# The last pair's memory stage in its own order, and the expert slots opened one attention group sooner

## The chip, the cores and the metric

One core of a Trainium2 chip runs the whole program. Its engines are TensorE (matmuls, called PE in the rows; PEld is its weight load), VectorE (DVE), ScalarE (ACT) and GpSimd (POOL); SyncE (SP) issues most transfers. Each engine works through its own queue strictly in the order of the program, and waits for others by semaphores. The metric is the device time of one execution in microseconds (us), the median of three runs.

## The reference

Eight batches with eight heads of 576 tokens attend to 32 memory slots per head; the 4608 output rows of 512 go through a top-1 mixture of eight experts. Cut to what matters:

```python
a = softmax(phi, axis=tokens)                       # phi: [8, 8, 576, 32]
k_m, v_m = a^T k, a^T v                             # "memory": 32 rows of 64 per head
attn = softmax(q k_m^T / sqrt(64)) v_m              # [8, 8, 576, 64]
x = attn as [4608, 512]
e_idx = argmax(x @ w_gate); gate_w = its softmax probability
eom = sigmoid(x @ w_output_gate)
out[mask_e] = gate_w * eom[:, e] * (relu(x[mask_e] @ w1[e]) @ w2[e])
```

## The kernel before

**Attention stage.** The batches go in four pairs (`bp` 0 to 3). For each pair the generator `memory(bp)` computes k_m and v_m (and v_m times the gate weights) from nine chunks of 128 tokens, for the two batches ("halves") of the pair. The order of its steps is a hand-written tuple, one letter and a number per step: `a` turns chunks of phi (TensorE transposes, ScalarE copies), `s` adds chunks to the sums in PSUM (32 small matmuls for a pair of chunks, 8 and 9 being the two parts of the last chunk), `p` spreads a finished half, `t` transposes it, `g` and `v` make its gate columns, `x` is a step of the next pair's softmax, and `.` gives the word back to the attention loop. `MEM0` orders pair 0 and `MEM` all others.

The loop `attention()` walks 20 groups (five per pair, of 256 tokens of four heads twice, the fifth of 64) through stages that lag each other: scores one group ahead (`C`, line 838), subtract the maximum, exponential, divide, transpose back (`B`), and values three groups later (`V`, line 899), stored to DRAM (line 1002). Each letter of `ORDER` is one step, and some of them take a step of memory or of routing along.

**Routing.** When a pair's logits are there, `rank` numbers its tokens per expert. After pair 1 `route_early` makes the early list (table "a": compares on VectorE at line 232, 72 small matmuls on TensorE at line 242, then indices), from which slots 0 to 3 gather their tokens. After pair 3 `route_late` makes the late list (table "l", 144 matmuls). `hold(n)` keeps a step back for n ticks of a program-time clock; `LATE` has those numbers for the time when slots are open.

**Expert stage.** A slot is up to 576 tokens of one expert. Its tokens come by five indirect row gathers issued by GpSimd (line 441), are transposed by TensorE (lines 1136, 1141) and split into a high and a low part (line 1099), as are the weights (ScalarE line 537, VectorE line 542). Slots 0 to 2 run as `plain`: 16 banks of 12 matmuls each (line 1310), evicted by ScalarE (1276) and VectorE (1281), and then the second layer (line 1442), five output tiles. Between banks a `hook` takes three attention steps and two of routing along, until attention is through.

Where the experts begin, and where the pools of routing are closed, is set by these lines:

```python
while t == START - 2 and stream.split(2):      # first weights are split
yield "open" if w == "S" and t == START else None   # the slots begin here
if t == START - 1:
    mem.finish()
if (i, step) == OPEN:                          # (2, 2): slot 2, third hook
    reopen()                                   # late.finish(), pools close
```

Of the kernel before, what the change touches and what calls it, by code (L numbers as in the profile page):

```python
# [19 lines left out]
NBP = B // 2  # L20
# [16 lines left out]
LAG = {"X": 1, "B": 2, "D": 1, "V": 3, "C": -1}  # L37
TICK = 0
HOOK = (3, 2)
START = 17  # L40
SWAP = ()
NKV = 8
NQ = 3
# [3 lines left out]
NLD = 2  # L47
MEM = ("a8", "a0", ".", "a2", ".", ".", "s0", ".", "a4", "s2", "x", "x", ".", ".", "s8", ".", "p0", "a6", ".", "x", ".", "s4", "x", "t0", ".", ".", "s9", "g0", "v0", ".", "s6", ".", "x", ".", "p1", "x", ".", "t1", ".", ".", "g1", "v1", ".")
MEM0 = ("a0", "s0", ".", "a2", "a8", ".", "s2", ".", "s8", "p0", "a4", ".", ".", "t0", ".", "g0", "a6", ".", "v0", "s9", "s4", ".", "s6", ".", ".", "p1", ".", "t1", "x", "x", ".", "g1", "x", ".", "v1", "x", ".", "x", ".", "x", ".", ".")
NPK = 1  # L50
PHI1 = 6
NEA = 3
LATE = {"lg": 8, "w": 2, "pe": 3, "dve": 2}
GROW = ((4, 0, 0), (2, 0, 0), (0, 2, 0))
SOON = {"pe": 3, "dve": 0, "tab": 12, "w": 3, "ix": 2}
PACE = 30
# [27 lines left out]
def attention_moe(tc, phiT, kv, qT, wgo, wall, out):  # L84
# [3 lines left out]
    with contextlib.ExitStack() as ctx:  # L88
# [134 lines left out]
        def table(nm, q, nch, nblk):  # L223
# [12 lines left out]
            yield from take_pr()  # L236
            yield from hold(LATE["pe"], SOON["tab"])
            pi = ps_r.tile([P, NBL], F32, name="pr")
# [5 lines left out]
            yield  # L244
            yield from hold(LATE["dve"], SOON["ix"])
            i2 = rt.tile([P, NBL], F32, name="i2")
# [9 lines left out]
        def route_early(n_):  # L256
# [27 lines left out]
            def slots_early():  # L284
# [6 lines left out]
                known(*order[0:NPE])  # L291
                yield from hold(LATE["w"], SOON["w"])
                stream.fetch()
# [96 lines left out]
        def take_pr():  # L390

            while taken:
                yield
            taken.append(1)

        def hold(n, soon=0):

            end = clock[0] + (n if "open" in env else soon)
            while clock[0] < end:
                yield  # L400
# [60 lines left out]
        def known(*zs):  # L461
            for z in zs:
                z["known"] = True
# [131 lines left out]
        ld = pl.enter_context(tc.tile_pool(name="ld", bufs=2, side="right"))  # L595
        ps_k = prr.enter_context(tc.tile_pool(name="ps_k", bufs=NPK, space=PSUM))
        pso = contextlib.ExitStack()
        env["pa"] = pso.enter_context(tc.tile_pool(name="pa", bufs=3 - NPK, space=PSUM))
        env["pd"] = pso.enter_context(tc.tile_pool(name="pd", bufs=2, space=PSUM))
# [66 lines left out]
        def soften(bp):  # L666

            ph = phs[bp]
            nmx = sm.tile([P, 4], F32, name="nmx")
            ssum = sm.tile([P, 4], F32, name="ssum")  # L670
            o = (0, 2, 1, 3)
            for i in range(5):
                if i < 4:
                    x = o[i]
                    V.tensor_reduce(nmx[:, x:x + 1], ph[:, x], axis=AX.X, op=ALU.max, negate=True)
                    tick()
                if i:
                    x = o[i - 1]
                    A.activation(ph[:, x], ph[:, x], AF.Exp, bias=nmx[:, x:x + 1], accum_out=ssum[:, x:x + 1])
                yield  # L680
            rs = sm.tile([P, 4], F32, name="rs")
            V.tensor_scalar(rs[:], ssum[:], 1e-9, None, ALU.add)
            V.reciprocal(rs[:], rs[:])
            rss[bp] = rs
            yield

        def memory(bp):
# [5 lines left out]
            a8 = ld.tile([P, 2, 256], F32, name="a8", bufs=1)  # L693
# [4 lines left out]
            def turn_a(*chunks):  # L698
                pt = bank([2, 256])
                for k, c in enumerate(chunks):  # L700
                    for g in range(2):
                        o = 512 if c == 8 else c * P + (c // 4) * P
                        T.transpose(pt[:, k, g * P:(g + 1) * P], exg[:, g, o:o + P], ident[:])
                c = chunks[0]
                turned.remove(c)
                if not turned and bp + 2 < NBP:
                    load_phi(bp + 2)
                if c == 8:
                    A.copy(a8[0:64, 0], pt[0:64, 0])
                    A.copy(a8[64:128, 1], pt[64:128, 0])  # L710
                else:
                    t = ld.tile([P, 2, 256], F32, name="at", bufs=NAT)
                    A.copy(t[:], pt)
                    at[c], at[c + 1] = t[:, 0], t[:, 1]
# [6 lines left out]
            def sums(c):  # L721

                b = 1 if c in togo[1] else 0
                if len(togo[b]) == 3:
                    z[b]["pk"] = ps_k.tile([P, 2, 2 * D], F32, name="pk")
                    T.matmul(z[b]["pk"][:].rearrange("p g d -> p (g d)"), zero[:, 0:P], zero[:],
                             start=True, stop=False)
                pk = z[b]["pk"]
                for ca_ in (c,) if c >= 8 else (c, c + 1):
                    for g in range(2):  # L730
                        for h in range(4):
                            T.matmul(pk[32 * h:32 * h + 32, g],
                                     at[ca_][:, g * P + 32 * h:g * P + 32 * h + 32],
                                     kvts[bp, min(ca_, 8)][:, 4 * g + h],
                                     start=False, stop=False)
                togo[b].remove(c)
                if not togo[b]:
                    T.matmul(pk[:].rearrange("p g d -> p (g d)"), zero[:, 0:P], zero[:], start=False, stop=True)
                if c < 8:
                    lod.step()  # L740
                elif b and bp + 1 < NBP:
                    load_kv(bp + 1, 8)

            def spread(b):

                z[b]["kv"] = kvm = ld.tile([P, 2, 2 * D], F32, name="kvm", bufs=2)
                z[b]["ve"] = wk.tile([P, 2, XQ], F32, name="ve_b", bufs=4)
                for g in range(2):
                    A.activation(kvm[:, g], z[b]["pk"][:, g], AF.Copy, scale=rs[:, 2 * g + b:2 * g + b + 1])
                h2 = [P, 2, 2, D]  # L750
                G.tensor_tensor(z[b]["ve"][:, :, 0:P].rearrange("p g (h d) -> p g h d", h=2),
                                kvm[:, :, D:2 * D].unsqueeze(2).to_broadcast(h2),
                                hmask[:].unsqueeze(1).unsqueeze(3).to_broadcast(h2), ALU.mult)
# [26 lines left out]
            def room():  # L780

                while len(ves) >= 4 + 2 * len(left):
                    yield

            soft = soften(bp + 1) if bp + 1 < NBP else iter(())
            for w in MEM if bp else MEM0:
                c = w[1:]
                if w == ".":
                    yield
                elif w[0] == "a":  # L790
                    turn_a(*((8,) if c == "8" else (int(c), int(c) + 1)))
                elif w[0] == "s":
                    sums(int(c))
                elif w[0] == "p":
                    yield from room()
                    spread(int(c))
                elif w[0] == "t":
                    turn_kv(int(c))
                elif w[0] == "g":
                    gates(int(c))  # L800
                elif w[0] == "v":
                    gates2(int(c))
                elif w == "x":
                    next(soft, None)
# [98 lines left out]
        def rank(bp, lg):  # L903
# [55 lines left out]
            def main():  # L959
                yield from take_pr()  # L960
                yield from hold(LATE["pe"], SOON["pe"])

# [10 lines left out]
                yield  # L973
                yield from hold(LATE["dve"], SOON["dve"])
                V.tensor_tensor(w1_[:], oh, pr[:, 0:NCH], ALU.mult)
# [171 lines left out]
        def defer(nm, f):  # L1147
            deferred.append([LATE[nm], f])

# [14 lines left out]
        def attention():  # L1164
# [8 lines left out]
            for t in range(NT + LAG["V"]):  # L1173
                for w in ORDER:
# [8 lines left out]
                    elif w == "W":  # L1183

                        while t == START - 2 and stream.split(2):
                            pass
# [29 lines left out]
                    clock[0] += 1  # L1216
                    yield "open" if w == "S" and t == START else None
                g = t - LAG["V"]
                if g >= 0 and g % 5 == 4:
# [6 lines left out]
                    else:  # L1226
                        late.gens.append(rank(bp, lgs[bp]))
                if t == START - 1:
                    mem.finish()
# [285 lines left out]
        def settle():  # L1515
# [6 lines left out]
            grow(1)  # L1522
            env["ps"] = prp.enter_context(tc.tile_pool(name="p1", bufs=7 - NPK, space=PSUM, reuse_waits="tile"))

# [59 lines left out]
        pso = contextlib.ExitStack()  # L1584
        env["ps"] = pso.enter_context(tc.tile_pool(name="p0", bufs=5 - NPK, space=PSUM, reuse_waits="tile"))
        env["pd"] = pso.enter_context(tc.tile_pool(name="pd1", bufs=1, space=PSUM, reuse_waits="tile"))
# [55 lines left out]
```

## Time and profile before

| | |
|---|---|
| median of 3 runs | 541.02 us (540.85 to 543.61) |
| profiled execution, its own time | 543.56 us |
| its span, first to last instruction | 541.6 us, so 2.0 us lie around it |
| TensorE busy | 506.0 us, 93% |
| VectorE, ScalarE, GpSimd busy | 375.6, 280.9, 164.8 us |
| mean granted TensorE clock | 0.964 of full |
| DMA | 104.01 MB, mean 192 GB/s |

The profile is of one execution; its time is that of the slowest of the three runs, and its rows are read for durations and order. The share of an engine is an average over the attention stage, in which TensorE has idle time, and the expert stage.

### The profile page before, as it was taken

Reading aid. Unit: us, or ns where it says so; the run is one execution under the profiler, and the core shown is the slowest. Engines: PE = TensorE matmul, PEld = TensorE weight load, DVE = VectorE, ACT = ScalarE, POOL = GpSimd, SP = SyncE. Lnnn points to the kernel's source line nnn. Section 1 sums busy time; section 2 is a strip of 40 time slices with the busy share of each in tenths; the row PEclk is TensorE's granted clock in tenths of the full one; section 3 lists DMA queues with packets and bytes.
Section 4 is the critical chain, followed back from the end, with each engine's and each line's share of the span. In section 5 each row is a group of like instructions: output and inputs, shape, how many; then the busy total and the mean of one; then the engine's idle time right before and its main releaser. Section 6 shows DMA issues by size and latency. Waiting matters only on the chain. (4 is left out here: it accounts for less than half of the span.)

```text
span 541.6 us, 11081 instructions
## 1 busy us (share of the span) xinstructions
PE 506.0 (93%) x4205; PEld 429.5 (79%) x4205; DVE 375.6 (69%) x870; ACT 280.9 (52%) x535; POOL 164.8 (30%) x168
## 2 busy tenths in 40 slices
PE   3788886989999999999999999999999999999995
PEld 2455554769877898789988988998898899889983
DVE  4374889787942698545593898688789878978600
ACT  4475764265533453244264756665574666548311
POOL 2242554543421330214146114302621341130021
PEclk9977998599999999999999999999999999999999
DMA  8999999888353664218407832980594188130011
GB/s 317 424 392 386 413 412 398 289 308 254 128 170 110 213 224 125 88 50 322 87 12 229 268 78 72 304 209 8 178 267 133 45 292 216 36 95 34 0 50 45
DMA packets 42111, 104.01 MB, mean 192 GB/s; under 512 B 4992, under 2 KB 16576, under 8 KB 41664
## 3 DMA queue, kind: packets, MB, share of 16 engines
q1 hardware_dynamic: 36160, 83.15, 46.0%
q0 software_dynamic: 5888, 20.06, 10.8%
q8 instruction: 35, 0.57, 0.4%
q14 instruction: 28, 0.23, 0.1%
HBM read 77.23 MB, written 20.05 MB: 180 GB/s over the span
## 5 line engine op out<-in xcount | busy, mean ns | idle before, releaser
L1442 PE MATMUL bps<-whl,hh 128*128 128x512 f32 x560 | 170.4, 398 | 0.0
L542 DVE TENSOR_TENSOR whl<-w,whl 128x1024 fp32r<-128x1024 f32 x74 | 90.7, 1233 | 48.6 <-ACT whl L537 40.2
L1442 PEld LDWEIGHTS bps<-whl,hh 128*128 128x128 f32 x560 | 104.7, 188 | 24.7
L1442 PE MATMUL bps<-whl,hl 128*128 128x512 f32 x216 | 85.4, 395 | 0.0
L537 ACT CAST whl<-w 128x1024 fp32r<-128x1024 f32 x74 | 76.8, 1049 | 4.3 <-PE bpc L1442 2.8
L1310 PE MATMUL bps<-xh,whl 128*128 128x288 f32 x384 | 77.6, 298 | 0.0
L1310 PEld LDWEIGHTS bps<-xh,whl 128*128 128x128 f32 x384 | 61.5, 188 | 1.3 <-DVE gr L1061 0.4
L1267 POOL DMA_INDIRECT out<-y,idx_oa x20 | 26.0, 1300 | 105.3 <-ACT y L1266 80.9
L1310 PE MATMUL bps<-xl,whl 128*128 128x288 f32 x192 | 54.8, 296 | 0.0
L1267 POOL DMA_INDIRECT out<-y,idx_ol x20 | 22.7, 1137 | 104.0 <-ACT y L1266 70.5
L1338 PE MATMUL bpc<-xh,whl 128*128 128x288 f32 x240 | 49.4, 296 | 0.0
L1338 PE MATMUL bpc<-th,whl 128*128 128x288 f32 x240 | 49.3, 295 | 0.0
L1442 PEld LDWEIGHTS bps<-whl,hl 128*128 128x128 f32 x216 | 40.7, 188 | 9.3
L1266 ACT ACTIVATE y<-bps,gx 128x512 f32<-128x512 f32 x27 | 18.6, 689 | 44.7 <-PE bps L1442 39.8
L1276 ACT ACTIVATE hh<-bps 128x288 fp32r<-128x288 f32 x48 | 19.7, 411 | 39.9 <-PE bps L1310 38.8
L1338 PEld LDWEIGHTS bpc<-xh,whl 128*128 128x128 f32 x240 | 38.9, 188 | 0.2
L1338 PEld LDWEIGHTS bpc<-th,whl 128*128 128x128 f32 x240 | 39.0, 188 | 0.0
L1276 ACT ACTIVATE hh<-keep 128x288 fp32r<-128x288 f32 x60 | 26.7, 445 | 22.7 <-DVE keep L1349 22.7
L901 ACT COPY xo<-bpd 128x576 f32<-128x576 f32 x36 | 22.2, 641 | 28.1 <-issue 9.5
L1310 PEld LDWEIGHTS bps<-xl,whl 128*128 128x128 f32 x192 | 35.6, 188 | 0.2
L857 POOL TENSOR_TENSOR ea<-ea,mx 128x512 f32<-128x512 f32 (+1 forms) x18 | 17.6, 977 | 59.5 <-DVE mx L855 51.3
L1338 PE MATMUL bpc<-tl,whl 128*128 128x288 f32 x120 | 35.4, 295 | 0.0
(246 smaller groups left out, 950.3 us busy)
## 6 DMA issues: line engine op xcount, KB each, us to landing
w<-wall SPq DMA_DIRECT2D x64, 512.0 KB
kvt<-kv SPq DMA_DIRECT2D x32, 512.0 KB
xs<-xo SPq DMA_DIRECT2D x16, 576.0 KB
qt<-qT SPq DMA_DIRECT2D x16, 512.0 KB
ph<-phiT SPq DMA_DIRECT2D x3, 1152.0 KB
xq<-xg SPq DMA_DIRECT2D x40, 80.0 KB
xq<-xg SPq DMA_DIRECT2D x40, 64.0 KB
kv<-kv SPq DMA_DIRECT2D x4, 512.0 KB
```

Of the source, the lines that this page charges most:

```text
L537: A.copy(hl[:, 0], w[:])
L542: V.tensor_tensor(hl[:, 1], w[:], hl[:, 0].bitcast(F32), ALU.subtract)
L857: (V if z["k"] in BESIDE[0] else G).tensor_tensor(eav, eav, mx[:, 0:n].unsqueeze(2).to_broadcast([P, n, M]), ALU.subtract)
L901: A.copy(xo[:, c % 2], px[:, :, 0:2 * XQ])
L1266: A.activation(y[0:n], py[0:n], AF.Copy, scale=z["g"][0:n, k:k + 1])
L1267: G.indirect_dma_start(out=out, out_offset=bass.IndirectOffsetOnAxis(ap=z["idx"][1][0:n, z["q0"] + k:z["q0"] + k + 1], axis=0), in_=y[0:n] ...
L1276: A.activation(h_[:, j, c:e], src, AF.Relu)
L1310: T.matmul(pb, w[:, b, o:o + P], x[a][:, cc, c * SL // 2:(c + 1) * SL // 2], start=(n == 0), stop=(n == 11))
L1338: T.matmul(pb, w[:, b, o:o + P], z[x][a][:, kc], start=(first and n == 0), stop=(n == 5), skip_group_check=not first)
L1442: T.matmul(py, a, w[:, b, DM * f:DM * f + DM], start=(u == 4 and f == 0 and n == 0), stop=(u == 7 and f == 1 and n == len(ps) - 1))
```

## The change

Three numbers or orders change. Pair 3 gets a tuple `MEM3` of its own: without the softmax steps of a next pair, with fewer pauses, and with `s9`, `s4` and `t0` in an earlier place. `START` goes from 17 to 16, so the slots open one group sooner and one group more is done in the hooks of slot 0. `LATE["pe"]` goes from 3 to 5 ticks, for the matmuls of `rank` and of the late table. As one line is added, line numbers of the change are one higher.

```diff
-START = 17
+START = 16
...
+MEM3 = ("a8", "a0", ".", "a2", ".", ".", "s0", ".", "a4", "s2", ".", "s8", ".", "p0", "a6", ".", "s9", "s4", "t0", ".", "g0", "v0", "s6", ".", "p1", ".", "t1", ".", "g1", "v1", ".")
...
-LATE = {"lg": 8, "w": 2, "pe": 3, "dve": 2}
+LATE = {"lg": 8, "w": 2, "pe": 5, "dve": 2}
...
-            for w in MEM if bp else MEM0:
+            for w in MEM3 if bp == NBP - 1 else MEM if bp else MEM0:
```

The order that it replaces for pair 3 (the `x` steps do nothing there):

```python
MEM = ("a8", "a0", ".", "a2", ".", ".", "s0", ".", "a4", "s2", "x", "x", ".", ".", "s8", ".", "p0", "a6", ".", "x", ".", "s4", "x", "t0", ".", ".", "s9", "g0", "v0", ".", "s6", ".", "x", ".", "p1", "x", ".", "t1", ".", ".", "g1", "v1", ".")
```

**Place 1.** TensorE ahead of the early list's table (the rows of Aw), in pair 3's memory stage; before. `ph` is phi, `at` and `a_1279` its turned chunks, `kvt` and `kv_1147` chunks of k and v, `pk` the sums, `kvm` a spread half.

```order
L732 MATMUL pk<-kvt,at 32x128 x16
L899 MATMUL bpd<-ve_b,aT 128x144 x8
L732 MATMUL pk<-kv_1147,a_1279 32x128 x8
L738 MATMUL pk<-zero 128x256
L703 MATMUL bpa<-ident,ph 128x128 x4
L838 MATMUL bpd<-qt,kT_177 32x64 x8
L838 MATMUL bpd<-qt,kT_178 32x64 x8
L242 LDWEIGHTS Aw
```

The same place of the change:

```order
L733 MATMUL pk<-kvt,at 32x128 x16
L733 MATMUL pk<-kv_1147,a_1279 32x128 x8
L739 MATMUL pk<-zero 128x256
L900 MATMUL bpd<-ve_b,aT 128x144 x8
L704 MATMUL bpa<-ident,ph 128x128 x4
L727 MATMUL pk<-zero 128x256
L733 MATMUL pk<-kv_1147,a_1279 32x128 x8
L733 MATMUL pk<-kvt,at 32x128 x16
L759 MATMUL bpa<-ident,kvm 128x128 x2
L839 MATMUL bpd<-qt,kT_177 32x64 x8
L839 MATMUL bpd<-qt,kT_178 32x64 x8
L243 LDWEIGHTS Aw
```

The second half's first sums (chunk 9, chunks 4 and 5) and the first half's transposes have come ahead of the table.

**Place 2.** TensorE from the end of the table to slot 0's first token transposes (`xg` are the gathered tokens); before, with the zero matmul's rows left out.

```order
L899 MATMUL bpd<-ve_b,aT 128x144 x8
...
L732 MATMUL pk<-kvt,at 32x128 x16
L758 MATMUL bpa<-ident,kvm 128x128 x2
L838 MATMUL bpd<-qt,kT_179 32x256 x8
L732 MATMUL pk<-kv_1147,a_1279 32x128 x8
L772 MATMUL bpa<-wg,vT_b 32x16 x8
L899 MATMUL bpd<-ve_b,aT 128x144 x8
L732 MATMUL pk<-kvt,at 32x128 x16
...
L899 MATMUL bpd<-ve_b,aT 128x144 x8
L772 MATMUL bpa<-wg,vT_b 32x16 x8
L838 MATMUL bpd<-qt,kT_180 32x256 x8
L1136 MATMUL bps<-ident,xg 128x128 x4
```

The same place of the change:

```order
L773 MATMUL bpa<-wg,vT_b 32x16 x8
L733 MATMUL pk<-kvt,at 32x128 x16
...
L900 MATMUL bpd<-ve_b,aT 128x144 x8
L839 MATMUL bpd<-qt,kT_179 32x256 x8
L759 MATMUL bpa<-ident,kvm 128x128 x2
L773 MATMUL bpa<-wg,vT_b 32x16 x8
L900 MATMUL bpd<-ve_b,aT 128x144 x8
L839 MATMUL bpd<-qt,kT_179 32x256 x8
L1137 MATMUL bps<-ident,xg 128x128 x4
```

One group's values and one group's scores are gone from here (they follow inside slot 0), and the sums of place 1. In SyncE's queue the second two weight loads now stand right behind the second store after the table, ahead of one load of q and one store.

**Place 3.** VectorE at the compares of the late list (`eql`), which TensorE's 144 matmuls read; before, where they stand at the end of slot 1.

```order
L378 TENSOR_TENSOR q_3063<-q_3063,q_3104 128x36
L232 TENSOR_TENSOR eql<-iota_bl,q_3063 128x864 x4
L542 TENSOR_TENSOR whl<-w,whl 128x1024
L1080 MEMSET lx 64x16
L1081 TENSOR_REDUCE lx<-xg 64x16
```

In the change, where they stand among slot 2's first evictions:

```order
L1282 SCALAR_TENSOR_TENSOR hl<-bps,hh 128x288
L1052 TENSOR_REDUCE gr<-lx 128x5
L1053 TENSOR_TENSOR ex<-iota_s,slot 128x8
L233 TENSOR_TENSOR eql<-iota_bl,q_3093 128x864 x2
L1282 SCALAR_TENSOR_TENSOR hl<-bps,hh 128x224
L1282 SCALAR_TENSOR_TENSOR hh<-bps,hh 128x64
L1055 TENSOR_TENSOR lx<-lx,gr 128x5x8
L1056 TENSOR_TENSOR lx<-lx,ex 128x5x8
L233 TENSOR_TENSOR eql<-iota_bl,q_3093 128x864 x2
L1282 SCALAR_TENSOR_TENSOR hl<-bps,hh 128x288
L250 TENSOR_SCALAR idx_gl<-pr 128x48
```

On TensorE the 144 matmuls now stand behind slot 2's third bank, 36 matmuls into the slot; before they stood inside slot 1's second layer.

## Rows read from the trace of the kernel before

**Rows 1.** Windows: stretch, length, busy of PE, PEld, DVE, ACT, POOL; clock, DMA share, GB/s.

```profile
118.08:238.50 120.42, 119.54 (x950) 103.84 (x949) 78.26 (x222) 50.17 (x89) 32.04 (x29) 1.00 0.48 154
238.50:500.00 261.50, 261.50 (x1540) 235.58 (x1539) 205.95 (x400) 155.76 (x282) 78.80 (x61) 1.00 0.51 151
90.00:93.00 3.00, 1.21 (x41) 0.87 (x38) 2.97 (x8) 1.89 (x5) 2.27 (x2) 0.97 1.03 422
94.00:109.00 15.00, 13.72 (x215) 10.30 (x218) 10.63 (x30) 4.49 (x9) 7.25 (x7) 0.50 0.83 293
110.00:114.50 4.50, 3.38 (x66) 1.77 (x50) 4.42 (x9) 3.65 (x10) 1.37 (x2) 1.00 1.02 406
```

**Rows 2.** Timeline of TensorE ahead of the experts: start us, length, engine, line, operation.

```profile
94.66 2.10 PE L242 MATMUL pr<-eqa,Aw 128*64 128x20 bf16 x72 [3.45 <-DVE eqa L232]
97.02 2.29 PE L899 MATMUL bpd<-ve_b,aT 64*128 64x144 f32 x16 [0.27 <-DVE idx_ga L249]
...
99.57 1.94 PE L732 MATMUL pk<-kvt,at 128*32 128x128 f32 x32
...
113.35 0.67 PE L838 MATMUL bpd<-qt,kT 64*32 64x256 f32 x16
114.54 0.66 PE L1136 MATMUL bps<-ident,xg 128*128 128x128 f32 x4 [0.52 <-DVE ve_b L777]
...
118.08 1.45 PE L1310 MATMUL bps<-xh,whl 128*128 128x288 f32 x8
```

**Rows 3.** Timeline of GpSimd: first and last row gather of slot 0.

```profile
98.24 1.41 POOL L441 DMA_INDIRECT xg<-xs,idx_ga  x1 [0.17 <-DVE mx L855]
...
104.12 0.97 POOL L441 DMA_INDIRECT xg<-xs,idx_ga  x1 [0.30 <-issue]
```

**Rows 4.** DMA queues in the stretch 98.2 to 103.7: packets, MB, share.

```profile
q1 hardware_dynamic: 593, 1.77, 96.4%
```

**Rows 5.** DMA queues in the stretch 103.7 to 111.2.

```profile
q1 hardware_dynamic: 584, 1.58, 57.4%
q0 software_dynamic: 368, 1.33, 44.4%
```

**Rows 6.** The page of the profiled execution: its span and instruction count.

```profile
span 541.6 us, 11081 instructions
```

**Rows 7.** Timeline of SyncE's DMA issues: kv chunks, a store, slot 0's second weights.

```profile
85.35 1.07 SPq L644 DMA_DIRECT2D kvt<-kv  x2
...
100.01 0.38 SPq L1002 DMA_DIRECT2D xs<-xo  x1
...
108.96 1.38 SPq L495 DMA_DIRECT2D w<-wall  x2
```

**Rows 8.** Timeline of VectorE: its first read of slot 0's tokens.

```profile
116.27 0.25 DVE L1081 TENSOR_REDUCE lx<-xg 64x16 f32<-64x64 f32 x1
```

**Rows 9.** Timeline of TensorE inside slot 0: attention's scores, values and rank.

```profile
127.32 0.66 PE L838 MATMUL bpd<-qt,kT 64*32 64x256 f32 x16
...
132.89 0.76 PE L899 MATMUL bpd<-ve_b,aT 64*128 64x144 f32 x8
...
136.50 0.19 PE L967 MATMUL pr<-ohg,strict 128*128 128x72 bf16 x1 [0.37 <-DVE ohg L927]
```

**Rows 10.** Timeline of the late list's table: TensorE's matmuls.

```profile
224.01 1.91 PE L242 MATMUL pr<-eql,Aw 128*64 128x48 bf16 x94
226.38 0.98 PE L242 MATMUL pr<-eql,Aw 128*64 128x48 bf16 x50 [0.46 <-issue]
```

**Rows 11.** Timeline of VectorE: late list's compares, then slot 2's first evictions.

```profile
217.45 3.96 DVE L232 TENSOR_TENSOR eql<-iota_bl,q 128x864 bf16<-128x864 bf16 x4
...
243.97 0.45 DVE L1281 SCALAR_TENSOR_TENSOR hl<-bps,hh 128x288 fp32r<-128x288 f32 x1
...
246.34 0.46 DVE L1281 SCALAR_TENSOR_TENSOR hl<-bps,hh 128x288 fp32r<-128x288 f32 x1 [0.82 <-issue]
```

**Rows 12.** DMA queues in the stretch 118.6 to 127, slot 1's gather.

```profile
q0 software_dynamic: 367, 1.33, 55.3%
```

## The prediction

> **What bounds the kernel now.** I read the stretches first. From 118.08 us on, TensorE is busy 119.54 of 120.42 us and then 261.50 of 261.50 us, at a granted clock of 1.00 [rows 1]: the expert stage is a queue of matmuls that nothing else holds up. So the span is made of two numbers: when the first expert matmul starts (118.08 us [rows 2]), and how much TensorE work stands in the program behind it, attention's leftovers included. A change ahead of the expert stage is worth what it does to the first; attention work pushed behind that start is paid in full in the second.
>
> Next, TensorE's instructions before 118 us in order of time [rows 2]. It waits 3.45 us for VectorE's comparison masks, runs the 72 small matmuls of the list's table at 94.66, then attention and memory matmuls of the last pair, and at 114.54 the transposes of slot 0's tokens. The stretch 94 to 109 has a granted clock of 0.50 (the 1.2 GHz level); 90 to 93 had 0.97 with TensorE busy for 1.21 of 3 us, and at 110 it is 1.00 again [rows 1].
>
> Last, the transfer that slot 0 needs. GpSimd issues the five row gathers from 98.24 to 105.09 [rows 3]. From 98.2 to 103.7 not one packet of its queue moves while SyncE's queue moves 1.77 MB; from 103.7 to 111.2 the gather's 1.33 MB pass beside 1.58 MB of SyncE's [rows 4, 5]. So the tokens are in SBUF at about 111.2, which is 3.3 us before TensorE asks for them at 114.54. Until then the end of this stage is set by the order of TensorE's queue, and below that lies the gather as a floor.
>
> **The change, part by part.** I start from the profiled execution (543.56 us, span 541.6 [rows 6]); the median of the runs is 541.02, 2.5 us less, so I add the sum to the median.
>
> *Work moved ahead of the table.* Chunk 9's sums, those of chunks 4 and 5 and the transposes of the first half's memory now stand ahead of the table (chunk 8's were ahead of it already and only pass a group's values). Chunks 4 and 5 took TensorE 1.94 us at the halved clock [rows 2]; with the rest I estimate under 3 us, inside the 3.45 us in which it waits for VectorE, so I cost them at nothing. That cover goes if their inputs are late: the last sums need two kv chunks whose loads were issued at 85.35 [rows 7], and the table stands behind them. Each microsecond by which those sums end after 94.66 would move the table. I take 0; the bound is 1 us, since GpSimd's own queue holds the gather until 98.24 (idle 0.17 before it [rows 3]).
>
> *Slots opened one group sooner.* Between the table and the transposes TensorE now lacks one group's values (2.29), the sums that moved (1.94) and one group's scores (0.67) [rows 2]: 4.9 us, so its queue would reach the transposes at 114.54 - 4.9 = 109.6. The gather is not there yet. The weight loads of slot 0's second pair move too: in SyncE's queue they went out at 108.96; now they stand directly behind the store of 100.01, two transfers sooner [rows 7], so 1.05 MB more compete with the gather. Bounds: nothing, because SyncE's queue was never empty in 103.7 to 111.2 anyway, and 2.7 us, if all of it goes first at the 0.39 MB/us of that stretch (1.58 + 1.33 MB in 7.5 us [rows 5]). I take 0.8, near the shared row. From VectorE's first read of the tokens (116.27 [rows 8]) to the first expert matmul it was 1.8 us. So the new start is 111.2 + 0.8 + 1.8 = 113.8: **-4.3 us**, with -6.8 (gather early, as below) and -1.6 as ends.
>
> The Trainium skill ("DMA: Bandwidth & Descriptors", section on queues, rings and completion order) says that each DMA engine round-robins between the queue rows it has work for. By that the gather shares from its first descriptors on (99.65, the end of its first instruction [rows 3]): at half of 0.39 MB/us its 1.33 MB would be over by 106.5, and the sum would be that of the first rival below. The trace agrees for 103.7 to 111.2 and does not for the 5.5 us before; my sum goes by the trace.
>
> *The group left behind.* One group more of attention now runs inside slot 0: values twice 0.76 and scores 0.66 [rows 9], at a TensorE that is hardly idle there (0.88 of 120.42 us [rows 1]): **+2.2 us**. Its VectorE, ScalarE and GpSimd work goes with it; VectorE was busy 78.26 of 120.42 us there [rows 1], and the banks hide an eviction that is late, so I add nothing. In GpSimd's queue slot 1's gather now stands ahead of one division and one subtraction; their readers on VectorE come about six evictions later, so again nothing.
>
> *"pe" from 3 to 5.* Rank and table matmuls wait two clock steps longer in the program. Rank's matmuls cost an idle 0.37 us at 136.50 waiting for VectorE [rows 9]; two steps more should remove that: **-0.3 us** (ends 0 and -0.4).
>
> *The late list's table.* Routing starts later by one group, and the list's table waits two steps longer. Before, its 144 matmuls stood late in slot 1, long after VectorE's four compares (3.96 us from 217.45), and idled 0.46 us [rows 10, 11]. Now the reopening of the pools at slot 2's third hook finishes it by force: two compares behind slot 2's first eviction, two behind the second, the table right after the third bank. VectorE's first and third eviction of slot 2 were at 243.97 and 246.34 [rows 11]. With 2.0 us of compares after the first, the second ends at about 247.3, and the last compare, after some small gate operations, at 249.5. The third bank was done about 0.6 us before its eviction, 245.7. The last quarter of the table (2.9 / 4 = 0.7 us [rows 10]) then ends at 250.2 where, unhindered, the table would end at 248.6. That is a wait of 1.6 in place of 0.46: **+1.2 us**, ends 0 and +3.
>
> *TensorE's clock at the start.* With less in its queue, TensorE has little to do while the gather lands (some 104 to 111 us). The nearest rows are 90 to 93, busy for 1.21 of 3 us and followed by 0.50, and 110 to 114.5, busy for 3.38 of 4.5 and at 1.00 [rows 1]. The first is nearer, so I expect the transposes and perhaps the first expert matmuls at 1.2 GHz, until the dense work brings the clock back. Ends: 0, and 2.5 us (5 us at half rate). I take **+0.9**.
>
> Sum: -4.3 + 2.2 - 0.3 + 1.2 + 0.9 = -0.3, so 541.02 - 0.3 = **540.7 us**: no change that can be told from none. A measurement of this kernel can tell about 0.5%, 2.7 us, from no change. The first expert matmul comes four microseconds sooner, and nearly all of it is paid back.
>
> **Rivals.**
> *Faster, the gather is early.* Slot 1's gather, in a quiet queue, moved its 1.33 MB within 118.6 to 127 [rows 12], 8.4 us from its first issue; the same from 98.24 is 106.6. If SyncE's store after the table comes late, as the values now stand behind more sums, the queue ahead of the gather empties sooner and it may come near that. Filling the 3.45 us may also keep TensorE at 2.4 GHz through 94 to 109 (15 us at 0.50 before), and then the engines' own chains end at about 111.3, so the start is -6.8, the clock term is 0 and the list's table costs 0.5: -6.8 + 2.2 - 0.3 + 0.5 = -4.4, **536.6 us**. For it: the halved clock came right behind that idle time. Against: the four transfers ahead of the gather are the same as before. Chance 0.27. The round-robin rule of the Trainium skill (the same page) would lead to this case too.
>
> *Slower, the clock stays down.* Before, a short idle time was followed by 15 us at 0.50, though TensorE was busy 13.72 of them [rows 1]. If the idle time while the gather lands does the same to the expert stage, 15 us there lose 7.5: -4.3 + 2.2 - 0.3 + 1.2 + 7.5 = +6.3, **547.3 us**. It decides from about 8 us at half rate on. Against: the expert matmuls are the densest work in the program, and no stretch of them shows less than 1.00. Chance 0.10. The Trainium skill ("TensorE: Matmul & The Clock Gate", part 1) says that an array that is kept busy returns to the full clock, as these rows show too.
>
> *The start does not move.* If the sums ahead of the table wait for their kv chunks, or the weights pass the gather in full, the start is 116.5 or later and the costs remain: -1.6 + 2.2 - 0.3 + 1.2 + 0.9 = +2.4 or a little more, **543.4 us**. For it: the DMA engines are saturated there (0.83 and 1.02 shares [rows 1]). Chance 0.13, split evenly by the 0.5% line.
>
> **How the numbers follow.** My forecast has 0.50 and spans about 538.5 to 542.8 by its own unknown terms. Faster by over 0.5%: most of the first rival and the forecast's lower edge, 0.27. Slower: 0.10 and half of 0.13, less what stays small, 0.15. Within: 0.58. For 8 in 10 the range takes in the first rival's middle and the case of a start that does not move: 536.8 to 543.6.
>
> **What would show it.** First expert matmul at about 113.8; last packet of slot 0's gather at 111 to 112; the table still at 94.7; values twice and scores once more inside slot 0; an idle TensorE of about 1.6 us, in pieces, at the table early in slot 2; a granted clock below 1.00 around 105 to 114. I am wrong if the gather ends before 109, if the table moves, if VectorE falls behind in slot 0 so that TensorE idles there, or if a low clock reaches past 118 us.

## The result, and the profile after

The change takes 543.37 us against 540.99 (medians of 20 executions each): a ratio of 1.0051, 95% interval 1.0034 to 1.0068, so by the ratio **2.8 us slower (1.8 to 3.7)**; the two medians differ by 2.4. Forecast were 540.7 us and no change.

The windows of the change, in the same stretches and columns as [rows 1]:

```profile
118.08:238.50 120.42, 119.59 (x834) 102.39 (x833) 74.94 (x217) 53.34 (x92) 31.05 (x30) 1.00 0.46 147
238.50:500.00 261.50, 260.96 (x1666) 235.02 (x1665) 209.05 (x406) 153.72 (x280) 75.37 (x60) 1.00 0.52 154
90.00:93.00 3.00, 1.96 (x50) 1.29 (x50) 2.86 (x9) 1.12 (x4) 1.64 (x2) 1.00 1.03 421
94.00:109.00 15.00, 10.01 (x206) 6.81 (x205) 13.18 (x33) 7.49 (x15) 8.41 (x8) 0.78 0.86 301
110.00:114.50 4.50, 3.25 (x18) 3.14 (x18) 2.40 (x6) 2.13 (x4) 0.75 (x1) 0.50 1.02 395
```

The expert stage is still a queue of matmuls, so the span is again the start plus the TensorE work behind it. The timeline of TensorE ahead of the experts answers to [rows 2]:

```profile
93.96 1.22 PE L243 MATMUL pr<-eqa,Aw 128*64 128x20 bf16 x67 [0.24 <-DVE eqa L233]
96.53 0.26 PE L243 MATMUL pr<-eqa,Aw 128*64 128x20 bf16 x5 [1.35 <-issue]
...
104.00 0.41 PE L773 MATMUL bpa<-wg,vT_b 64*32 64x16 f32 x16 [2.87 <-ACT vT_b L765]
...
109.55 0.48 PE L1137 MATMUL bps<-ident,xg 128*128 128x128 f32 x1 [0.88 <-DMA xg<-xs,idx_ga]
111.27 0.66 PE L1142 MATMUL bps<-ident,xg 64*128 64x64 f32 x4 [1.25 <-DMA xg<-xs,idx_ga]
...
114.33 2.08 PE L1311 MATMUL bps<-xh,whl 128*128 128x288 f32 x8
```

The moved sums fill the wait at the table (3.45 us before, 0.24 now), but with a gap of 1.35 us inside it the table ends at 96.79, where it ended before (96.76). (A releaser "issue" means that the engine waited for nothing that the profile shows.) The transposes now wait for the gather itself, and the first expert matmul stands at 114.33 in place of 118.08, at 1.2 GHz (its first 8 matmuls take 2.08 us, those of before 1.45 [rows 2]). DMA queues of the change from 97.5, where the gather is first issued, to 102.5, and from there to 111:

```profile
q1 hardware_dynamic: 527, 1.57, 92.7%
...
q0 software_dynamic: 368, 1.33, 39.9%
```

As in [rows 4, 5], no packet of the gather moves in the first five microseconds, and all of it in the next eight. (By the round-robin rule of the Trainium skill, "DMA: Bandwidth & Descriptors", section on queues, rings and completion order, it would have shared from its first descriptors on; the trace disagrees in this kernel too, if these stood when the first gather instruction ended, at 98.78, which no row shows.)

The timeline of TensorE in slot 2 answers to [rows 10]:

```profile
237.26 0.40 PE L1311 MATMUL bps<-xh,whl 128*128 128x288 f32 x1 [0.83 <-ACT y L1267]
...
242.23 1.32 PE L243 MATMUL pr<-eql,Aw 128*64 128x48 bf16 x72
243.84 0.75 PE L243 MATMUL pr<-eql,Aw 128*64 128x48 bf16 x36 [0.29 <-DVE eql L233]
244.84 0.75 PE L243 MATMUL pr<-eql,Aw 128*64 128x48 bf16 x36 [0.24 <-DVE eql L233]
```

The late list's table stands where it was forecast, in pieces, over in 3.36 us. Slot 2's first bank waits 0.83 us, which nobody forecast. Span less start is 541.3 - 114.33 = 427.0 us; before it was 423.5. Between these two executions (543.32 and 543.56 us, by their own times) the sum of -0.3 came out, by terms that partly cancel. Between the medians it did not.

### The profile page after: what moved, and what is told of

Its sections match the earlier page's. It is cut to its first block, busy times and chain, and to the rows that moved or that the text cites. A ratio compares the mean times of both kernels' runs of the same rounds, so it can differ in the third digit from the quotient of the medians.

```text
span 541.3 us, 11084 instructions
## 1 busy us (share of the span) xinstructions
PE 503.6 (93%) x4205; PEld 427.8 (79%) x4205; DVE 375.5 (69%) x870; ACT 281.0 (52%) x535; POOL 161.4 (30%) x168
## 5 line engine op out<-in xcount | busy, mean ns | idle before, releaser
L1268 POOL DMA_INDIRECT out<-y,idx_ol x20 | 20.8, 1038 | 104.7 <-ACT y L1267 70.4
L1339 PE MATMUL bpc<-xl,whl 128*128 128x288 f32 x120 | 35.1, 293 | 0.0
```

What stands on the lines that cost most here:

```text
L1268: G.indirect_dma_start(out=out, out_offset=bass.IndirectOffsetOnAxis(ap=z["idx"][1][0:n, z["q0"] + k:z["q0"] + k + 1], axis=0), in_=y[0:n] ...
L1339: T.matmul(pb, w[:, b, o:o + P], z[x][a][:, kc], start=(first and n == 0), stop=(n == 5), skip_group_check=not first)
```

## Experiments

All are compared with the kernel before on the same chip; b1 and b2 are one execution each. The table gives, for each whole kernel, the median, the difference by the ratio's interval, and from its one profiled execution the own time, the first expert matmul, and span less that start.

| kernel | median us | against before | own time | start | rest |
|---|---|---|---|---|---|
| before, first profile | 540.99 | | 543.56 | 118.08 | 423.5 |
| a1 before again | 541.30 | -0.2 (-1.1 to 0.6) | 542.70 | 118.30 | 422.4 |
| b1 before again | | | 544.07 | 118.49 | 423.6 |
| b5 before, OPEN (2, 4) | 541.98 | 0.3 (-0.6 to 1.1) | 542.01 | 117.86 | 422.2 |
| a5 LATE pe 5 alone | 541.45 | 0.4 (-0.5 to 1.2) | 541.14 | 117.12 | 422.0 |
| a3 MEM3 alone | 542.47 | 1.2 (0.1 to 2.3) | 543.41 | 119.00 | 422.5 |
| b4 START 18 | 545.62 | 3.0 (1.9 to 4.1) | 545.63 | 122.09 | 421.7 |
| a2 START 16 alone | 544.49 | 2.4 (1.0 to 3.8) | 545.80 | 116.24 | 427.8 |
| a4 change, LATE pe 3 | 544.15 | 3.2 (1.8 to 4.5) | 541.22 | 112.78 | 426.5 |
| change, first profile | 543.37 | 2.8 (1.8 to 3.7) | 543.32 | 114.33 | 427.0 |
| d1 change again | 543.91 | 2.3 (1.0 to 3.6) | 543.12 | 113.73 | 427.6 |
| b2 change again | | | 547.53 | 113.93 | 431.6 |
| b3 change, OPEN (2, 4) | 543.27 | 1.0 (0.1 to 1.8) | 542.50 | 114.14 | 426.4 |
| d4 the same again | 543.64 | 1.5 (0.3 to 2.8) | 544.84 | 116.61 | 426.3 |

**The parts apart.** a1 is the kernel before, unchanged. a2 makes one edit to it, a3 another (with the tuple `MEM3` of the change):

```diff
-START = 17
+START = 16
```

```diff
-            for w in MEM if bp else MEM0:
+            for w in MEM3 if bp == NBP - 1 else MEM if bp else MEM0:
```

a4 takes an edit back from the change; a5 (below) makes the same edit the other way round to the kernel before:

```diff
-LATE = {"lg": 8, "w": 2, "pe": 5, "dve": 2}
+LATE = {"lg": 8, "w": 2, "pe": 3, "dve": 2}
```

> The kernel before once more, unchanged, for a second profile and for the noise: ratio 1.000, within 0.997 to 1.003. Theory A (the first profile, at 543.6 us, was an execution with TensorE's clock down ahead of the experts, and the start of 118.08 us is not the usual one): in a profile near the median of 541 us the first expert matmul stands at 115 to 116.5 us, and from it to the end of the span it is 423.5 us as before. Theory B (the usual start is 118.1 and the 2.5 us lie behind it): the first expert matmul stands at 117.5 to 118.5 us again, and the rest is nearer 421 us.

> The kernel before with START 16 alone: the slots open one attention group sooner, order of the memory steps and LATE as before. Theory A (start held up by slot 0's gather at about 114 us, so that the usual gain is only 1 to 2 us, and the group that goes into slot 0 costs 2.2 us, the late list's table in slot 2 about 1): first expert matmul at 114 to 115.5, time +1.5 to +3.5 us, nearly all of the change's +2.8. Theory B (the loss is in the new memory order or in the two ticks more of the late matmuls): time within 1 us of before.

> The kernel before with the new memory order of pair 3 alone: START 17, LATE as before, so no group more runs inside slot 0. Theory A (the order ahead of the experts costs nothing and fills the wait at the table): first expert matmul at 115 to 116.5, the rest 423.5, time -1.0 to +0.5 us. Theory B (the new order is what costs): time +1.5 to +3 us.

> The change with LATE for rank's and the table's matmuls back at 3 ticks. Theory A (the two ticks are worth 0.3 us at most, and the late list's table stays where the reopening at slot 2's third hook puts it): +2.3 to +3.5 us against the kernel before, within 0.6 us of the change. Theory B (the two ticks push the late routing back and that is the loss): +0.5 to +1.5 us.

START 16 alone loses 2.4 us, about as much as the change; the two ticks are not the loss (a4). The new order alone does not help either. Its timelines, first ScalarE's, then TensorE's, show why it may cost:

```profile
111.88 0.64 ACT L902 COPY xo<-bpd 128x576 f32<-128x576 f32 x1 [2.75 <-DMA xs<-xo]
```

```profile
112.57 1.33 PE L900 MATMUL bpd<-ve_b,aT 64*128 64x144 f32 x8 [4.29 <-ACT xo L902]
```

The last group's values come out earlier than an earlier store has left its buffer, so what was saved at the table is given back 18 us later. That is one profile; a1 shows the same wait with 1.12 us. a1 did not settle the first question: an execution of 542.7 us, above its median, and again a start of 118.3.

**More profiles, a later opening, a later table.**

b1 and b2 are the kernel before and the change once more. b3 and d4 make the first of these edits to the change, b5 makes it to the kernel before; b4 makes the second to the kernel before:

```diff
-OPEN = (2, 2)
+OPEN = (2, 4)
```

```diff
-START = 17
+START = 18
```

> The kernel before, unchanged, for a third profile. From the first expert matmul to the end of the span it was 423.5 and 422.4 us in two profiles with starts of 118.1 and 118.3 and times of 543.6 and 542.7, both above the median of 541.2. Theory A: that stretch is 422 to 424 again, whatever the time, and the start follows the time: an execution of 541 starts its experts near 116. Theory B: the start is 118 to 118.5 whatever the time, and the stretch behind it is shorter in an execution of 541, near 421.

> The change, unchanged, for a second profile. Theory A: the first expert matmul 3 to 4 us behind the last packet of slot 0's gather (110.6 and 114.3 in the first profile), the rest 426.5 to 427.5. Theory B (low clock at the head of the expert stage is what makes the slow executions, up to 547.6): if the time is above 544.5, a granted clock below 1.00 reaches past the first expert matmul by 5 us or more, and the rest is 428 or more.

> The change with the reopening two hooks later, at slot 2's fifth hook, so that the late list's table stands behind five banks and not three. Theory A (the table's wait costs 0.5 us there): within 0.7 us of the change, +2 to +3 us against the kernel before. Theory B (the table forced at slot 2's third hook is the loss): +0.5 to +1.2 us against the kernel before.

> The kernel before with START 18: the slots open one attention group later, so one group fewer runs inside slot 0 and one more ahead of the experts. Theory A (in a usual execution the start is set by TensorE's queue, about level with the gather): start 2 to 3 us later, the rest 2.2 us shorter, time -0.3 to +1.2 us. Theory B (the start is set by something that a group of attention does not delay, the weights or the clock): start unchanged, time -1.5 to -2.5 us.

b4 lost more than either theory gave it: its start went to 122.09, 4 us later and not 2 to 3. Its rest is the shortest of all (421.7), 0.5 us less than b5's, and holds a low clock (0.62 granted over the first 3.91 us) that costs 1.5; together 2.0, near the 2.2 of the group. So 17 is the best of the three openings. b1 was late again. b2 was an execution of 547.53 us, and it shows where such a time goes. Its TensorE timeline at the late list's table, then a window in it:

```profile
242.48 0.91 PE L243 MATMUL pr<-eql,Aw 128*64 128x48 bf16 x45
243.87 0.27 PE L243 MATMUL pr<-eql,Aw 128*64 128x48 bf16 x5 [0.48 <-issue]
244.63 0.27 PE L243 MATMUL pr<-eql,Aw 128*64 128x48 bf16 x5 [0.49 <-issue]
245.37 0.26 PE L243 MATMUL pr<-eql,Aw 128*64 128x48 bf16 x4 [0.47 <-issue]
246.08 0.29 PE L243 MATMUL pr<-eql,Aw 128*64 128x48 bf16 x6 [0.46 <-issue]
246.82 2.31 PE L243 MATMUL pr<-eql,Aw 128*64 128x48 bf16 x79 [0.45 <-issue]
```

```profile
246.80:250.20 3.40, 3.38 (x84) 3.34 (x84) 0.63 (x4) 0.00 (x0) 0.00 (x0) 0.51 0.97 365
```

Five gaps of nearly half a microsecond in which TensorE waits for nothing that the profile shows, and behind them the 1.2 GHz level for 3.4 us, into the expert matmuls: the table takes 6.65 us (242.48 to 249.13) in place of 3.36. Theory B of that run named the low clock at the head of the stage; that is there too (0.50 from 113.93 to 117.10), but the larger part lies at the table. Where the table meets no stall, as in b5, it takes 2.46:

```profile
223.35 2.46 PE L242 MATMUL pr<-eql,Aw 128*64 128x48 bf16 x144
```

With the reopening two hooks later the table takes 2.46 us in d4 as well (3.00 in b3, with one gap of 0.34), and b3's difference to the kernel before is that of its theory B. Of 24 executions of b3 and d4 none is above 544.9 us; of 33 of the change 12 are above 545.0 (of 123 of the kernel before, 3). The medians of d1 and d4, on one chip, differ by 0.3 us, as d4's text (below) expected where the table usually costs what it did in the first profile; the means differ by 0.8 (544.29 and 543.49).

A stalled table is not the only way to such a time. Five of d4's twelve executions stand at 544.6 to 544.8, and the one profiled of them (544.84) started late and met no stall at the table; so did a2 (545.80), whose table stands where the change's does. TensorE in d4, then in a2:

```profile
113.54 0.66 PE L1142 MATMUL bps<-ident,xg 64*128 64x64 f32 x4 [0.77 <-DMA xg<-xs,idx_ga]
...
116.61 2.14 PE L1311 MATMUL bps<-xh,whl 128*128 128x288 f32 x8
...
247.74 2.46 PE L243 MATMUL pr<-eql,Aw 128*64 128x48 bf16 x144
```

```profile
116.24 2.27 PE L1310 MATMUL bps<-xh,whl 128*128 128x288 f32 x8
...
244.58 1.32 PE L242 MATMUL pr<-eql,Aw 128*64 128x48 bf16 x72
246.20 0.75 PE L242 MATMUL pr<-eql,Aw 128*64 128x48 bf16 x36 [0.29 <-DVE eql L232]
247.19 0.75 PE L242 MATMUL pr<-eql,Aw 128*64 128x48 bf16 x36 [0.24 <-DVE eql L232]
```

**Cut kernels.** The program ends behind slot 0's twelfth bank; the rest is left out:

```diff
+CUT = (0, 3)
...
+class Cut(Exception):
+    pass
...
+                if (i, u) == CUT:
+                    raise Cut
...
-        run(stream)
+        try:
+            run(stream)
+        except Cut:
+            pso.close()
+            pm.close()
+            return
```

> The kernel before, cut off behind slot 0's twelfth bank: everything that stands behind it in the program is left out, so the output is not written. Its time is the start of the experts plus twelve banks and the attention steps between them, about 155 us, and its median over many executions says where the start usually lies, which one profile can't. Theory A (the profiles of before, with starts of 118.1 to 118.5, are executions that started late): the profiled execution is 1.5 us or more above the median of the others. Theory B (118 is the usual start): the profiled execution lies within 0.5 us of the median.

> The change, cut off at the same bank. Its slot 0 holds about 0.4 us less attention work up to there. Theory A (the usual start moves by 1 to 2 us only, the full costs stand behind): median 1 to 2.5 us below the cut kernel before. Theory B (the start moves by the 4.2 us between the two kernels' profiles, and what is lost is lost later, at the list's table in slot 2): median 3.5 to 5 us below it.

> The new memory order alone (START 17), cut off at the same bank. It took +1.2 us as a whole kernel, and nothing behind the start differs. Theory A (the order delays the start, because the last groups' values wait longer for their stores): +0.5 to +1.5 us against the cut kernel before. Theory B (the +1.2 lies elsewhere): within 0.4 us of it.

> START 16 alone, cut off at the same bank, with about 0.4 us less attention work up to there, as in the change. Theory A: 0.5 to 2 us below the cut kernel before (as a whole kernel it took +2.4, with 3.5 to 4 us of costs behind the start). Theory B: 2.5 us or more below it, as the one profile has it (116.2 against 118.1 to 118.5).

> The change, unchanged, timed on the same chip as the two cut kernels and as the change with the later reopening. Theory C (the start moves by 3 to 3.5 us; behind it 2.2 us for the group, 0.8 for slot 2's first bank, 0.5 us or more for the list's table, 0.5 to 1 for the clock): +0.7 to +1.8 us against the kernel before. Theory D (in the usual execution of before the start is near 116, which its profiles miss): +2.3 to +3.5 us.

> The kernel before cut off behind slot 0's twelfth bank, on the chip on which the whole kernels are timed. In profiles the end lies 389 to 390 us behind the end of this cut kernel (its trailing work taken into account), whatever the start. Theory C: median of the whole kernel before less median of this one is 388.5 to 390.5 us. Theory D: it is 387 us or less.

> The change cut off at the same bank. Its trailing work behind the last bank is 1.4 us shorter. Theory C: 4.3 to 5.2 us below the cut kernel before, so a start that moves by 2.9 to 3.8 us; the whole change less this one 394 to 395.5 us. Theory D: the start moves by 2 us or less, so at most 3.4 us below.

> The change with the reopening two hooks later, beside the change on one chip. If the list's table behind slot 2's third bank often meets stalls like the five issue gaps of 0.47 us and the 3.4 us of low clock in the second profile of the change: 1 to 2 us below the change. If it usually costs the 0.5 us of the first profile: 0.2 to 0.6 us below.

| cut kernel | median us (range) | median of those within 1.5% of the quickest |
|---|---|---|
| c1 before | 153.38 (152.43 to 153.68) | 153.38 (5 of 5) |
| d2 before | 152.78 (151.69 to 153.84) | 152.78 (5 of 5) |
| c2 change | 148.60 (147.37 to 155.20) | 148.37 (5 of 6) |
| d3 change | 148.40 (145.99 to 153.75) | 146.34 (3 of 6) |
| c3 MEM3 alone | 153.98 (153.03 to 154.49) | 153.98 (5 of 5) |
| c4 START 16 alone | 150.04 (147.09 to 152.87) | 147.09 (1 of 6) |

VectorE has 1.4 us more to finish behind the last matmul in the cut kernel before (8.5 us to the end of the span against 7.1 in the profiles of c1 and c2). Less that, the start moves by 4.8 - 1.4 = 3.4 us from c1 to c2 and by 4.4 - 1.4 = 3.0 from d2 to d3. Beside d2 and d3, the whole kernels differ by 543.91 - 541.53 = 2.4 us. Between cut and end lie 543.91 - 148.40 = 395.5 us in the change and 541.53 - 152.78 = 388.75 before; the difference of 6.8 less 1.4 says that **the work behind the start grew by about 5 us** (5.4 by these medians). Five or six executions stand behind each cut median, and those of the change spread by 7.8 us in c2 and in d3, so these readings are no better than a microsecond or two: by the last column the start moves by 3.6 and 5.0 us and the work grows by 7.4, by the means of all cut executions (152.99 and 149.32) the start moves by 2.3, and in the whole kernels' profiles, b2 aside, the rest grows by 3.4 to 5.6. By the medians neither theory took it all: the start is C's, the loss is D's. c4 lies 3.3 us below c1, 1.9 without the trailing work, but its range overlaps c2's and d3's; c3 lies 0.6 us above c1 with overlapping ranges. So the order's own cost, and what it is worth at START 16, stay unsettled.

The question put to c1 came out for its theory B: the profiled execution lies 0.3 us above the median, that of d2 on it, and they start at 118.87 and 118.88. So in the cut kernels 118 is no late start. c2's profile, 0.2 us above its median, starts at 116.47, which is 2.4 us sooner. Before's profiles start later cut than whole (118.08 to 118.49); why, no run shows. And much of the change's spread arises ahead of the cut, where no late table stands: three of its twelve executions lie 3.9 to 6.6 us above their medians, of the ten of before none lies more than 1.1 above.

> The kernel before with LATE 5 in place of 3 for rank's and the late table's matmuls alone. Nothing ahead of the experts differs, so its start is a further sample of before's. Theory (the two ticks are worth between 0.4 us gained and nothing): -0.6 to +0.3 us. Rival (they push the late list's table back towards slot 2 and cost): +0.5 us or more, with the table behind 228 us. Start: 118 to 119 if before's profiles show the usual start; 116 to 117.3 in an execution of 541.5 us or less if the usual start is earlier than theirs.

> The kernel before with the reopening two hooks later. TensorE, VectorE, ScalarE and GpSimd have the same instructions in the same order (the list's table is over in slot 1 there), so both theories expect no change, within 0.5 us, and its start is one more sample of before's: from the end of the twelfth bank to the end 398.5 to 399.6 us as in the four profiles so far, and the first expert matmul near 117 us in an execution of 541.5 us, near 118.3 in one of 543.

These two have the kernel before's instructions ahead of the experts, and gave the executions near the median that were missing: the timelines of a5 and b5 at the first expert matmul.

```profile
117.12 1.60 PE L1310 MATMUL bps<-xh,whl 128*128 128x288 f32 x8
```

```profile
117.86 1.45 PE L1310 MATMUL bps<-xh,whl 128*128 128x288 f32 x8
```

In a5 the late list's table stands at 229.71, nearer slot 2, and takes 2.46 us there too. No version beat the kernel before.

## Why the prediction was wrong, step by step

**What held.** The start is set by the gather and not by TensorE's queue in three profiles of the change, at 114.3, 113.7 and 113.9 us, forecast 113.8. (In b3 and c2, at 114.14 and 116.47, the transposes wait for VectorE, with the tokens there.) Weights ahead of the gather did not hold it up further: from its first issue to its last packet it takes 13.1 us (97.54 to 110.6), 12.8 before. The group left behind costs 2.2 us by its matmuls, at a TensorE that idles 0.83 of 120.42 us; b4 says 2.0. The granted clock is 0.50 from 102.40 to 116.06, past the start, which costs half of 1.7 us, 0.9. The table early in slot 2 comes in pieces.

That the start fits to half a microsecond is luck. The tokens were to be there at 112.0 and came at 110.6 to 111.3; and from VectorE's first read of them to the first expert matmul, 1.8 us in the sum, it took 3.17 (111.16 to 114.33), as the transposes run at 1.2 GHz too. a4, at the full clock there, takes 1.83. So the clock's term, forecast +0.9 for transposes and first matmuls together, is 2.2 in this profile: 1.3 ahead of the start and 0.9 behind it. VectorE's first read in the first profile and in a4, a4's first expert matmul, and the clocks, of a4 ahead of its start and of the first profile behind it:

```profile
111.16 0.25 DVE L1082 TENSOR_REDUCE lx<-xg 64x16 f32<-64x64 f32 x1 [1.25 <-DMA xg<-xs,idx_ga]
...
110.95 0.26 DVE L1082 TENSOR_REDUCE lx<-xg 64x16 f32<-64x64 f32 x1
...
112.78 1.46 PE L1311 MATMUL bps<-xh,whl 128*128 128x288 f32 x8
...
110.00:112.78 2.78, 2.04 (x17) 1.58 (x17) 2.71 (x8) 2.00 (x4) 1.05 (x1) 1.00 1.00 401
114.33:116.06 1.73, 1.73 (x9) 1.73 (x8) 1.38 (x2) 0.71 (x2) 1.04 (x1) 0.50 0.98 394
```

**What failed: "I add the sum to the median".** The sum was made against one execution of 543.56 us, and 2.5 of these are not in a usual one. About 0.6 may lie in its start (118.08; 117.5 is the mean of a5 and b5, whose times are near the median; the cut kernels, with 118.9 in a usual execution, do not bear this out), some 1.4 behind it (423.5 against 422.0 to 422.4). Of these, the two stalls that the rows showed account for 1.3: the wait of rank's matmul, 0.37 [rows 9], and the gap in the late table [rows 10], with which it took 3.35 us in place of 2.46. Of seven profiles with START 17 or 18 one has the first stall and two the second. A stall that a usual execution does not have cannot be saved in it, and cannot stand for a cost that is there already.

Term by term, against the usual execution:
- *Start, -4.3.* It is -3.5 by the profiles (114.0 against 117.5), -3.0 to -3.4 by the medians of the cut kernels and -2.3 by their means. The new start was right, by two errors that cancel, for an execution in which the gather is on time; it does not hold for the late ones (116.61 in d4, 116.47 in c2).
- *"pe" 3 to 5, -0.3.* Nothing: alone it is +0.4, no change within its interval. The wait of 0.37 that it was to remove is in none of a1, a5 and b5.
- *Late list's table, +1.2.* It was costed as a wait of 1.6 in place of 0.46. The waits were 0.53, but the usual table before has no stall, so the cost is 3.36 - 2.46 = 0.9 when all goes well, and 4.2 in b2, with the low clock behind it on top.
- *A term that was missing, +0.8.* The prediction followed the group's matmuls into slot 0 but not the end of attention. Before, attention ends inside slot 0 (its last values at 170.31) and the PSUM pools change hands at that slot's end, without a wait. Now the last values stand at 178.02, the end is not reached there, and the pools change hands at the end of slot 1, where slot 2's first bank waits for the last eviction of the old pool. This 0.82 or 0.83 us <-ACT y stands in all seven profiles of whole kernels with START 16 and in none of the seven with START 17 or 18. I did not undo it alone, so its share is read, not tested.

Start -3.5, group +2.2, slot 2's first bank +0.8, table +0.9, clock behind the start +0.7 (0.9 less 0.2, as before loses a third of a microsecond at its start in a5, where 2.00 us have 0.83, and none in b5) make +1.1. Measured are +2.3 and +2.8 by ratio, +2.5 and +2.6 by means. Two things can fill the difference of some 1.4 us. A table as slow as b2's adds 3.3 us and, by an estimate from its windows, half a microsecond of low clock behind it; if the 12 of 33 executions above 545 us are of that kind, that is 1.4 on the mean. But one of the twelve was profiled, and a2 and d4 have such times, or nearly, from late starts with no stall at the table. With the start moved by 2.3 us only, as the means of the cut kernels have it, the sum is +2.3 without any table like b2's. How much belongs to either stays open.

**The rivals.** "Faster, the gather is early" did not come: the gather's last packet is at 110.6, though the clock from 94 to 109 did rise, to 0.78 from 0.50. "The start does not move" gave 543.4, which is the time, but not by its mechanism: the start moved. "The clock stays down" named a mechanism that b2 shows, at another place and for 3.4 us. The Trainium skill ("Runtime: NRT & Kernel Launch", Instruction fetch mechanics) says that an engine's instructions are brought in by a DMA queue of its own, mostly hidden. b2's gaps show no sign of such a fetch: no packet of an instruction queue moves there from 242.6 to 249.4, while one does about the single gap of before (225.5 to 226.8). In b2 the DMA engines are busy 0.99 of the time over the gaps (243.4 to 246.8), in a5 0.03 and in b5 0.52 at a table without one. But the first profile of the change has 0.99 there too and no such gap (242.2 to 245.6), so a busy DMA alone doesn't make them; what an "issue" gap waits for, no run here shows.

**Left open.** Why before's profiles lie late: all three of the unchanged kernel are above 542.5 us. What makes a start of the change late; in d4 and c2 the early table already stands at 95.48 and 95.13 (93.96 in the first profile), but so it does in b2 (95.14), which started at 113.93. And how much of the loss would go if attention ended inside slot 0 again.

## What to carry to other kernels

A sum made from one profiled execution belongs to that execution. Where its time lies away from the median, look first for what is odd in it (an issue gap, a wait of a few tenths, a start that other profiles don't show; here the start was the doubtful one) and take it out before the sum is added to the median. A low clock that reaches past a start has also slowed what stands ahead of it, and costs in both places. And when work is pushed past a border, follow what is tied to its end (a pool that closes, a list that must be finished) as well as the work itself; a block of small matmuls that is forced between dense ones is worth a row of its own in the sum, with its bad executions.

## What was not expected of the hardware

- A dense stage can lose the full clock: granted 0.51 from 246.80 to 250.20 us in b2, behind five issue gaps (TensorE busy 1.09 of the 3.40 us before); in the first profile of before the two stretches of the expert stage show 1.00 [rows 1].
- "Issue" gaps come in sizes: 0.45 to 0.49 us after every 4 to 6 small matmuls in b2, 0.46, 0.47 and 0.34 once in the first profile [rows 10], b1 and b3, none in a1, a5, b5 and d4, and 1.35 inside the early table of the change (1.20 to 1.41 in a4, b3 and d1, none in b2 and d4), for the same kind of matmul.
